# Linear attention and two feed-forward layers on one core: all attention tiles ahead of the first softplus, on one PSUM bank each

## The chip, the core and the metric

The kernel runs on one core of a Trainium2 chip. The metric is the device time of one execution in microseconds. The kernel before takes 881.84 us (median of 3 runs, 880.49 to 882.64).

## What is computed

```python
kv  = einsum('bhsd,bhse->bhde', k, v)      # b=4, h=8, s=576, d=64
o   = einsum('bhsd,bhde->bhse', q, kv)
o   = o / sqrt(mean(o*o, axis=-1) + 1e-6) * g_norm
x   = o.transpose(0, 2, 1, 3).reshape(2304, 512)
x   = softplus(x @ w_in1) @ w_out1         # 512 -> 2048 -> 512
out = elu(x @ w_in2) @ w_out2              # 512 -> 2048 -> 512
```

All in float32. The norm needs a reciprocal square root for each token and head.

## The kernel before, in words

The 2304 tokens are 6 blocks of 384. The 16 chunks of hidden units are taken in quarters of four. A *slot* is one pair of token blocks with one pair of chunks: 7 products (Strassen's scheme) of 6 matmuls each, 42 in all (`product`, line 695), written to PSUM tags `h` (2 banks), `m` and `o` (1 each). ScalarE and VectorE copy and add the parts, apply the activation (`slot_act`) and split the result into a high and a low part (tile `G`). The output pieces (`slot_piece`, lines 879 to 881, always three matmuls together) of a group of two slots run during the two slots that follow. Each layer has 24 slots.

A slot's first operand is made from the block's 7 sums (`operands`, line 648 on ScalarE, and `low_part`, line 660 on VectorE). Tag `sx` has room for 7 of these operand tiles. Each is also written out to memory (a *spill*, line 665) and loaded again in the later quarters. The weights come as raw words (line 269), are converted (`conv`, lines 278 to 298) and split (`split`, `split_pair`, `split_sums`, lines 305 to 363).

Attention makes the token blocks. `kv_strand` loads k and v (lines 385 and 387) into parts of `acc_sb` and multiplies them (line 396). Block 0 is made by four `pair_strand`s, the other tokens by 15 `tile_strand`s of 128 tokens; both go through `attention` (lines 451 to 511): load q (line 458), products with kv into a PSUM bank (line 467), squares on ScalarE (line 473), row sums on VectorE (line 482), a reciprocal root, a multiply (line 489), transposes on TensorE (line 504), and a scaled copy into `acc_sb` (line 509).

The root of the four pairs uses ScalarE's Ln and Exp and a Newton step of four small VectorE instructions (`rsqrt`). When the last pair is through, ScalarE's table is changed to that of softplus, which has no Ln and Exp; so the 15 tiles take their root from integer arithmetic (`rsqrt_pool`: a seed on VectorE, lines 438, 441 and 443, and three Newton rounds of four GpSimd instructions, lines 446 to 449, reckoned as `12 * 150` ns). The tiles of block 1 (`direct`) keep one bank of tag `acc` from the products to the transposes; the 12 others copy the products to the q tile (line 476), give the bank of tag `o` back, and take it again for the transposes.

What sets the order: `Order.run` is a list scheduler that runs while the program is built. Each strand yields its next step with the engines it may run on, an estimate of its cost in ns, and what it needs; the step that can start first is issued, and a strand with a smaller key may hold others back (by at most `WAIT` = 300 ns, or 200 ns). So every engine has a fixed order, laid down from estimates. Three steps may go to VectorE or GpSimd: lines 293, 319 and 357 (with 360). Where TensorE would be idle before slot 1, `warm` puts dummy matmuls (line 932). All DMAs are issued by SyncE, in the order of the plan.

Of the kernel before, what the change touches and what calls it, by code (L numbers as in the profile page):

```python
# [16 lines left out]
P = 128  # L17

# [30 lines left out]
class Order:  # L49
# [119 lines left out]
def linear_attention_then_two_ffns(  # L169
# [21 lines left out]
    nc = tc.nc  # L191
# [56 lines left out]
    def on(engine):  # L248
        return {DVE: nc.vector, POOL: nc.gpsimd, ACT: nc.scalar}[engine]

# [13 lines left out]
    def conv(i):  # L264
# [27 lines left out]
        e = yield ((DVE, dve(512) + 90), (POOL, pool(512), BIAS_I)), []  # L292
        on(e).tensor_tensor(c, c, r, op=ALU.add)
# [11 lines left out]
    def split(i, n):  # L305
# [19 lines left out]
    def split_pair(i, n):  # L325
# [4 lines left out]
        yield ((DVE, dve(256)),), [ring("c"), ring("r"), ("split", n), ("q", i + 1)]  # L330
# [13 lines left out]
        order.add(order.now, split_sums(layer, fc, ct, ct_h, rt, rt_h))  # L344
        yield from split(i + 1, n + 1)

    def split_sums(layer, fc, ct, ct_h, rt, rt_h):
        yield ((ACT, act(512)),), [ring("wx")]
        wx, wx_h = sbuf("wx", 2, f"wx{layer}_{fc}", (P, 2, 3, 256), F32R)
# [6 lines left out]
        e = yield ((DVE, dve(512)), (POOL, pool(512), BIAS_W)), []  # L356
        on(e).tensor_sub(wx[:, 1, 0::2, :], ct, f32(wx)[:, 0, 0::2, :])
        drop(ct_h)
        e = yield ((DVE, dve(256)), (POOL, pool(256), BIAS_W)), []
        on(e).tensor_sub(wx[:, 1, 1, :], rt[:, :256], f32(wx)[:, 0, 1, :])  # L360
        drop(rt_h)
        wx_t[layer, fc] = (wx, wx_h)
        mark("wx", layer, fc)


# [6 lines left out]
    def stage(b, c):  # L372

        return NB - NP + c if b < 2 else NB - 2 + c % 2

    def kv_strand(b, c):
        t = acc_sb[stage(b, c)]
        n, r = 4 * 2 * D2, S - 4 * P
        before = [
            ("kvmm", *k)  # L380
            for k in ((b0, c0) for b0 in range(B) for c0 in range(NP))
            if k < (b, c) and stage(*k) == stage(b, c)
        ]
        yield ((DMA, dma(4 * n * P)),), before
# [4 lines left out]
        tag = ("o", "acc", "m")[min(b, 2)]  # L389
# [13 lines left out]
        mark("kvmm", b, c)  # L403
        f = kvf[b % 2][:, c, :]
# [10 lines left out]
    ROOM = {"sx": 7, "wx": 2, "gx": 3}  # L415

    def rsqrt(ms, r, u, m, last):

        yield ((ACT, 100),), []
        nc.scalar.activation(r, ms, AF.Ln, scale=1.0 / D, bias=EPS)  # L420
        nc.vector.tensor_scalar(m, ms, 1.0 / D, EPS, op0=ALU.mult, op1=ALU.add)
        order.free[DVE] += 75
        yield ((ACT, 100),), []
        nc.scalar.activation(r, r, AF.Exp, scale=-0.5)
        if last:
            load_set(SOFTPLUS_SET)
        yield ((DVE, 75),), []
        nc.vector.scalar_tensor_tensor(u, r, -0.5, m, op0=ALU.mult, op1=ALU.mult)
        yield ((DVE, 75),), []
        nc.vector.tensor_mul(u, u, r)  # L430
        yield ((DVE, 75),), []
        nc.vector.scalar_tensor_tensor(r, u, 1.5, r, op0=ALU.add, op1=ALU.mult)

    def rsqrt_pool(ms, r, u, m):


        yield ((DVE, 75),), []
        nc.vector.tensor_scalar(m, ms, 1.0 / D, EPS, op0=ALU.mult, op1=ALU.add)
        yield ((DVE, 75),), []
        ub, rb = u.bitcast(U32), r.bitcast(U32)  # L440
        nc.vector.tensor_scalar(ub, m.bitcast(U32), 1, None, op0=ALU.logical_shift_right)
        yield ((DVE, 75),), []
        nc.vector.tensor_scalar(rb, ub, -1.0, float(0x5F3759DF), op0=ALU.mult, op1=ALU.add)
        yield ((POOL, 12 * 150),), []
        for _ in range(3):
            nc.gpsimd.tensor_mul(u, r, r)  # L446
            nc.gpsimd.tensor_mul(u, u, m)  # L447
            nc.gpsimd.tensor_scalar(u, u, -0.5, 1.5, op0=ALU.mult, op1=ALU.add)  # L448
            nc.gpsimd.tensor_mul(r, r, u)  # L449

    def attention(nm, load, products, n, tag, direct, parts):

# [4 lines left out]
        y = q.rearrange("p c t -> p (c t)")[:, :n]  # L457
# [3 lines left out]
            ring(tag),  # L461
# [7 lines left out]
        po = po[:, :n]  # L469
# [10 lines left out]
        small, small_h = sbuf("small", 3, f"small{nm}", (P, 4, H))  # L480
# [14 lines left out]

        if direct:
            yield ((PE, n // P * 109),), [("ident",)]
            pt, pt_h = bank, po_h
        else:
            yield ((PE, n // P * 109),), [ring(tag), ("ident",)]  # L500
            pt, pt_h = psum(tag, f"pt{nm}")
        for i in range(n // P):
            s = slice(i * P, (i + 1) * P)
            nc.tensor.transpose(pt[:, s], y[:, s], ident)
        drop(q_h)
        j, pt, x = parts(pt[:, :n])
        old = [("kvmm", b, c) for b in range(B) for c in range(NP) if stage(b, c) == j]
        yield ((ACT, act(n, True) + 90),), [("gn",), *old]
        nc.scalar.activation(x, pt, AF.Copy, scale=gn)  # L509
        drop(pt_h)  # L510
        mark("x", nm)

    def pair_strand(c):
# [12 lines left out]
        return attention(("pair", c), load, products, T, "acc", True, parts)  # L526

    def tile_strand(t):
# [20 lines left out]
        early = t < 2 * TT  # L549
        return attention(t, load, products, DM, "acc" if early else "o", early, parts)  # L550
# [107 lines left out]
    def low_part(layer, p, o, t, x, x_h):  # L658
# [48 lines left out]
    def slot_h(s, pieces):  # L707
# [40 lines left out]
        a, a_h = k["A"]  # L748
        order.add(key - URGENT, copy("ca", "hj", 1, 0))
# [37 lines left out]
    def softplus(s, b, h, a, ready):  # L787
        if a:
# [105 lines left out]
    BIAS_W = -1000  # L894
    BIAS_I = -400
# [5 lines left out]
    W_LEAD2 = 12  # L901
    A_LEAD = 12
    A_STEP = 1.2
    KV_LEAD = 2
    FIRST = -12
    CONV0 = -19.95
# [18 lines left out]
    def warm():  # L925

        p, p_h = psum("h", "warm")
        while entry[0] < base(1):
            yield ((PE, pe(P, 4)),), []
            if entry[0] < base(1):  # L930
                a = ident if ("x", ("pair", 0)) in order.marks else kvf[1][:, 0, :]
                nc.tensor.matmul(p[:, -P:], a, a, start=True, stop=True)
# [105 lines left out]
```

## Time and profile before

| | |
|---|---|
| median of the runs | 881.84 us |
| the profiled execution | 881.4 us |
| its span, first to last instruction | 879.6 us |
| TensorE busy | 832.4 us (95%) |
| VectorE busy | 619.0 us (70%) |
| ScalarE busy | 460.3 us (52%) |
| GpSimd busy | 66.3 us (8%) |
| mean granted TensorE clock | 0.979 |

In the profile PE is TensorE, PEld its weight loads, DVE is VectorE, ACT is ScalarE, POOL is GpSimd and SP is SyncE. Busy time is the time in which an instruction of the engine ran. Matmuls overlap, so their mean duration is longer than the distance from one to the next. The clock is granted as a share of 2.4 GHz; its two levels are 1.2 and 2.4 GHz.

### The profile page before, as it was taken

Reading aid. Unit: us, or ns where it says so; the run is one execution under the profiler, and the core shown is the slowest. Engines: PE = TensorE matmul, PEld = TensorE weight load, DVE = VectorE, ACT = ScalarE, POOL = GpSimd, SP = SyncE. Lnnn points to the kernel's source line nnn. Section 1 sums busy time; section 2 is a strip of 40 time slices with the busy share of each in tenths; the row PEclk is TensorE's granted clock in tenths of the full one; section 3 lists DMA queues with packets and bytes.
Section 4 is the critical chain, followed back from the end, with each engine's and each line's share of the span. In section 5 each row is a group of like instructions: output and inputs, shape, how many; then the busy total and the mean of one; then the engine's idle time right before and its main releaser. Section 6 shows DMA issues by size and latency. Waiting matters only on the chain.

```text
span 879.6 us, 12592 instructions
## 1 busy us (share of the span) xinstructions
PE 832.4 (95%) x4732; PEld 779.2 (89%) x4732; DVE 619.0 (70%) x1061; ACT 460.3 (52%) x781; POOL 66.3 (8%) x199
## 2 busy tenths in 40 slices
PE   7876687999999999999998999999999999999998
PEld 6775576999999999999997988888898888888887
DVE  4675676967636984589449999878559984995444
ACT  3564465666424553356235757676456643664431
POOL 0235544000000000000000000000000000000000
PEclk9996788999999999999999999999999999999999
DMA  6976262675664585377432765768538655744802
GB/s 204 316 265 241 87 263 92 266 254 181 237 251 147 213 336 195 120 281 288 175 139 85 287 242 189 278 213 307 193 115 307 225 213 184 280 156 151 310 37 107
DMA packets 43708, 185.36 MB, mean 211 GB/s; under 512 B 4992, under 2 KB 7808, under 8 KB 43648
## 3 DMA queue, kind: packets, MB, share of 16 engines
q1 hardware_dynamic: 43648, 184.57, 58.5%
q8 instruction: 37, 0.61, 0.3%
q14 instruction: 23, 0.19, 0.1%
HBM read 146.80 MB, written 37.75 MB: 210 GB/s over the span
## 4 chain that ended last, share of the span: by engine, by line
PE 79%; DVE 8%; POOL 6%; issue 2%; DMA 2%; ACT 2%; SPq 0%; POOLq 0%; DVEq 0%
PE A L695 20%; PE acc L880 14%; PE acc L881 14%; PE acc L879 14%; PE B L695 10%; PE C L695 5%; DVE x L660 2%; POOL small L447 2%; POOL small L449 2%; DMA acc_sb<-kv 2%; POOL small L446 1%; POOL small L448 1%; DVE q L489 1%; DVE acc_sb L642 1%; DVE acc_sb L569 1%
## 5 line engine op out<-in xcount | busy, mean ns | idle before, releaser
L879 PE MATMUL acc<-G,whi 128*128 128x384 f32 x384 | 129.6, 338 | 0.0
L881 PE MATMUL acc<-G,whi 128*128 128x384 f32 x384 | 128.9, 336 | 0.0
L880 PE MATMUL acc<-G,wlo 128*128 128x384 f32 x384 | 128.9, 336 | 0.0
L695 PE MATMUL A<-x,wx 128*128 128x384 f32 x576 | 118.1, 338 | 4.5 <-ACT x L648 2.6
L881 PE MATMUL acc<-wlo,G 128*128 128x512 f32 (+1 forms) x292 | 114.9, 393 | 0.0
L695 PE MATMUL A<-x,whi 128*128 128x384 f32 x384 | 113.2, 335 | 1.7 <-DVE x L660 1.7
L880 PE MATMUL acc<-whi,G 128*128 128x512 f32 (+1 forms) x292 | 114.4, 392 | 0.0
L879 PE MATMUL acc<-whi,G 128*128 128x512 f32 (+1 forms) x292 | 112.7, 386 | 0.0
L695 PEld LDWEIGHTS A<-x,wx 128*128 128x128 f32 x576 | 102.1, 189 | 10.9 <-ACT x L648 4.1
L733 DVE TENSOR_TENSOR hj<-hj,C 128x384 f32<-128x384 f32 x48 | 26.5, 553 | 71.6 <-PE C L695 71.3
L733 DVE TENSOR_TENSOR hk<-hk,B 128x384 f32<-128x384 f32 x48 | 26.5, 551 | 67.7 <-PE B L695 66.0
L695 PEld LDWEIGHTS A<-x,whi 128*128 128x128 f32 x384 | 70.7, 188 | 3.8 <-DVE x L660 2.0
L879 PEld LDWEIGHTS acc<-G,whi 128*128 128x128 f32 x384 | 72.7, 189 | 0.4 <-DVE acc_sb L569 0.2
L880 PEld LDWEIGHTS acc<-G,wlo 128*128 128x128 f32 x384 | 72.6, 189 | 0.0
L881 PEld LDWEIGHTS acc<-G,whi 128*128 128x128 f32 x384 | 72.5, 189 | 0.0
L315 ACT CAST whi<-q 128x512 fp32r<-128x512 f32 x64 | 39.6, 618 | 57.4 <-DVE q L297 32.6
L881 PEld LDWEIGHTS acc<-wlo,G 128*128 128x128 f32 x292 | 54.7, 187 | 11.3
L695 PE MATMUL A<-x,wlo 128*128 128x384 f32 x192 | 64.4, 335 | 0.0
L569 DVE TENSOR_TENSOR acc_sb<-acc_sb,acc 128x384 f32<-128x384 f32 (+1 forms) x108 | 62.3, 596 | 1.6
L695 PE MATMUL C<-x,whi 128*128 128x384 f32 x192 | 58.5, 346 | 3.3 <-ACT acc_sb L509 3.3
L879 PEld LDWEIGHTS acc<-whi,G 128*128 128x128 f32 x292 | 54.9, 188 | 6.0
L880 PEld LDWEIGHTS acc<-whi,G 128*128 128x128 f32 x292 | 54.8, 188 | 6.0
(151 smaller groups left out, 1594.2 us busy)
## 6 DMA issues: line engine op xcount, KB each, us to landing
x<-spill SPq DMA_DIRECT2D x126, 768.0 KB, 5.9
raw<-w SPq DMA_DIRECT2D x64, 512.0 KB, 5.5
spill<-x SPq DMA_DIRECT2D x42, 768.0 KB, 5.3
acc_sb<-kv SPq DMA_DIRECT2D x16, 512.0 KB, 5.4
out<-o SPq DMA_DIRECT2D x17, 256.0 KB, 2.0
q<-qt SPq DMA_DIRECT2D x15, 256.0 KB, 2.7
acc_sb<-kv_rest SPq DMA_DIRECT2D x16, 64.0 KB, 4.6
out<-o SPq DMA_DIRECT2D x2, 128.0 KB, 1.7
```

Source lines behind the costliest of these rows:

```text
L315: nc.scalar.copy(hi, q)
L446: nc.gpsimd.tensor_mul(u, r, r)
L447: nc.gpsimd.tensor_mul(u, u, m)
L448: nc.gpsimd.tensor_scalar(u, u, -0.5, 1.5, op0=ALU.mult, op1=ALU.add)
L449: nc.gpsimd.tensor_mul(r, r, u)
L569: nc.vector.tensor_add(a, a, p)
L660: nc.vector.tensor_sub(t[:, 2:, :], x, f32(t)[:, :2, :])
L695: nc.tensor.matmul(bank[:, :T], w, x, start=start and i == 0, stop=stop and i == len(seq) - 1, skip_group_check=True,)
L733: nc.vector.tensor_add(to, to, bank[:, :T])
L879: nc.tensor.matmul(a, l[0], r[0], start=(u == 0), stop=False)
L880: nc.tensor.matmul(a, l[1], r[0], start=False, stop=False)
L881: nc.tensor.matmul(a, l[0], r[1], start=False, stop=(u == QF - 1))
```

## The change

- All 19 tiles of attention take one path: Ln and Exp on ScalarE, then one Newton step of five GpSimd instructions (reckoned as `5 * 280` ns). The integer seed and the three rounds are gone. ScalarE's table is changed to softplus only when all 19 have their Exp issued; every softplus stands behind that.
- Every tile keeps one bank of tag `acc` (4 banks) from the products to the copy out. The copy to the q tile is gone; the q tile is free after the products, and the multiply reads PSUM and writes a tile of the `G` ring.
- k and v of batches 2 and 3 are loaded into the `gx` ring (3 tiles) and not into `acc_sb`; the kv products use tags `o` and `m` in turn.
- The attention strands get keys below those of the slots (`t - 20`), the first operands -14.5, weight chunks 2 and 3 -7.5. The spill of an operand gets a key of at least 1.
- Lines 293, 319, 357 and 360 run on VectorE alone.
- The dummy matmuls go on to slot 7 and are written to unused columns of the open slot's bank. The loads of later weights have other leads (8, and 12 more for some, where it was 12). The ring of `wx` is claimed earlier in `split_pair`.

The core of the diff:

```diff
@@ conv @@
-        e = yield ((DVE, dve(512) + 90), (POOL, pool(512), BIAS_I)), []
-        on(e).tensor_tensor(c, c, r, op=ALU.add)
+        yield ((DVE, dve(512) + 90),), []
+        nc.vector.tensor_tensor(c, c, r, op=ALU.add)
...
@@ split @@
-        e = yield ((DVE, dve(512)), (POOL, pool(512), BIAS_W)), [ring(f"wlo{half}")]
+        yield ((DVE, dve(512)),), [ring(f"wlo{half}")]
...
@@ kv_strand @@
+    def kv_room(b, c):
+        if b < 2:
+            return acc_sb[NB - NP + c], None
+        return sbuf("gx", ROOM["gx"], f"kv_sb{b}_{c}", (P, T * KC))
...
-        tag = ("o", "acc", "m")[min(b, 2)]
+        tag = "om"[c % 2]
...
@@ attention @@
-        po, po_h = psum(tag, f"po{nm}")
-        bank = po
+        bank, po_h = psum("acc", f"po{nm}")
         for b, c, rows, cols, lhs in products:
-            nc.tensor.matmul(po[rows, cols], lhs(q), kvf[b % 2][:, c, :], start=True, stop=True)
+            nc.tensor.matmul(bank[rows, cols], lhs(q), kvf[b % 2][:, c, :], start=True, stop=True)
+        drop(q_h)
...
-        if not direct:
-            yield ((ACT, act(n, True)),), []
-            nc.scalar.copy(y, po)
-            drop(po_h)
-            po = y
...
-        if isinstance(nm, tuple):
-            yield from rsqrt(ms, r, u, m, nm[1] == NP - 1)
-        else:
-            yield from rsqrt_pool(ms, r, u, m)
-        yield ((DVE, dve(n)),), []
+        yield ((ACT, 100),), []
+        nc.scalar.activation(r, ms, AF.Ln, scale=1.0 / D, bias=EPS)
+        yield ((ACT, 100),), []
+        nc.scalar.activation(r, r, AF.Exp, scale=-0.5)
+        roots.append(nm)
+        yield ((POOL, 5 * 280),), []
+        nc.gpsimd.tensor_scalar(m, ms, 1.0 / D, EPS, op0=ALU.mult, op1=ALU.add)
+        nc.gpsimd.tensor_mul(u, r, r)
+        nc.gpsimd.tensor_mul(u, u, m)
+        nc.gpsimd.tensor_scalar(u, u, -0.5, 1.5, op0=ALU.mult, op1=ALU.add)
+        nc.gpsimd.tensor_mul(r, r, u)
+        yield ((DVE, dve(n)),), [ring("G")]
+        y, y_h = sbuf("G", 4, f"y{nm}")
...
@@ low_part @@
+        order.rekey(max(order.now, SPILL))
         yield ((DMA, dma(P * 4 * T * 4)),), []
         nc.sync.dma_start(spilled[layer, p, o], f32(t))
...
@@ softplus @@
+        if s == 0 and a:
+            yield ((ACT, 1300),), [lambda: len(roots) == TILES]
+            load_set(SOFTPLUS_SET)
+            mark("softplus")
+        ready = [*ready, ("softplus",)]
...
-    W_LEAD2 = 12
-    A_LEAD = 12
-    A_STEP = 1.2
+    W_LEAD2 = 8
     KV_LEAD = 2
-    FIRST = -12
-    CONV0 = -19.95
+    FIRST = -14.5
+    SECOND = -7.5
+    SPILL = 1
+    WARM_SLOTS = 7
...
@@ warm @@
-        while entry[0] < base(1):
+        while entry[0] < base(WARM_SLOTS):
...
+                nc.tensor.matmul(
+                    (chain[0] if chain else p)[:, -P:], a, a, start=not chain, stop=not chain, skip_group_check=True
+                )
...
@@ the strands' keys @@
-            return n - (W_LEAD if n < base(FP * NPAIR) else W_LEAD2)
+            if n < base(FP * NPAIR):
+                return n - W_LEAD
+            return n - W_LEAD2 - (3 * W_LEAD if half and fc % QF < 2 else 0)
...
-            order.add(tile_key(t), tile_strand(t))
+            order.add(t - 20, tile_strand(t))
...
-                order.add(tile_key(b * S // P) - KV_LEAD + 0.1 * c, kv_strand(b, c))
+                order.add(b * S // P - 20 - KV_LEAD + 0.1 * c, kv_strand(b, c))
```

## Rows read from the trace of the kernel before

**Rows 1.** Windows: us, busy of PE, PEld, DVE, ACT, POOL, then clock, DMA, GB/s

```profile
0.00:30.00 30.00, 22.24 (x239) 18.93 (x240) 13.66 (x39) 12.68 (x32) 1.97 (x7) 0.94 0.73 237
70.00:80.00 10.00, 3.11 (x30) 2.16 (x29) 5.19 (x9) 4.44 (x9) 5.70 (x21) 0.59 0.42 146
0.00:160.00 160.00, 121.17 (x928) 107.94 (x929) 103.04 (x206) 84.50 (x164) 59.96 (x195) 0.88 0.60 206
160.00:200.00 40.00, 40.00 (x233) 40.00 (x232) 29.92 (x50) 26.11 (x45) 1.89 (x1) 1.00 0.75 282
200.00:300.00 100.00, 100.00 (x579) 100.00 (x578) 65.68 (x113) 47.31 (x84) 0.00 (x0) 1.00 0.60 214
470.00:530.00 60.00, 54.63 (x293) 50.70 (x292) 58.15 (x94) 38.05 (x60) 0.00 (x0) 1.00 0.60 229
```

**Rows 2.** Windows again, PE and PEld alone: line 695's matmuls, then line 879's

```profile
0.00:160.00 160.00, 36.92 (x159) 31.36 (x160) 0.88 0.60 206
...
0.00:160.00 160.00, 10.26 (x27) 5.65 (x27) 0.88 0.60 206
```

**Rows 3.** Waits of VectorE, 0 to 160 us: total, times, longest

```profile
DVE q L489 <- POOL small L449: 27.9, 15, 2.6
```

**Rows 4.** Chain of waits, 0 to 160 us, its shares by line

```profile
by line: issue 9.5%; POOL small L447 8.6%; POOL small L449 8.5%; DMA acc_sb<-kv 8.5%; POOL small L446 7.3%; POOL small L448 7.0%; DVE q L489 5.9%; DVE x L660 5.8%; DVE small L482 3.0%; PE pt L504 2.5%; DMA q('pair', 3)_265<-qt 1.9%; DVE q L
```

**Rows 5.** Timeline: GpSimd, one tile's first and last root step; VectorE, its multiply

```profile
39.69 0.19 POOL L446 TENSOR_TENSOR small<-small 128x8 f32<-128x8 f32 x1
...
43.08 0.20 POOL L449 TENSOR_TENSOR small<-small 128x8 f32<-128x8 f32 x1
...
43.31 0.69 DVE L489 TENSOR_TENSOR q<-po,small 128x512 f32<-128x512 f32 x1 [1.23 <-POOL small L449]
```

**Rows 6.** Groups of VectorE, 0 to 160 us: count, busy us, mean ns, idle before

```profile
L489 DVE TENSOR_TENSOR q<-q,small 128x512 f32<-128x512 f32 x12 | 11.4, 954 | 22.2 <-POOL small L449 22.2
L293 DVE CUSTOM_DVE_ANT_0 c<-c,r 128x1024 uint16<-128x1024 uint16 x7 | 4.8, 692 | 0.6
...
L438 DVE TENSOR_SCALAR small<-small 128x8 f32<-128x8 f32 x15 | 3.4, 237 | 0.1
L443 DVE TENSOR_SCALAR small<-small 128x8 uint32<-128x8 uint32 x15 | 3.1, 207 | 0.2
...
L441 DVE TENSOR_SCALAR small<-small 128x8 uint32<-128x8 uint32 x15 | 2.8, 198 | 0.1
...
L489 DVE TENSOR_TENSOR q<-po,small 128x512 f32<-128x512 f32 x3 | 2.1, 692 | 5.7 <-POOL small L449 5.7
...
L428 DVE SCALAR_TENSOR_TENSOR small('pair', 0)_188<-small('pair', 0)_188 128x6 f32<-128x6 f32 x1 | 0.2, 166 | 1.2 <-ACT small('pair', 0)_188 L424 1.2
```

**Rows 7.** Groups of GpSimd, 0 to 160 us

```profile
L447 POOL TENSOR_TENSOR small<-small 128x8 f32<-128x8 f32 x45 | 13.2, 294 | 3.5
...
L319 POOL TENSOR_TENSOR wlo<-q,whi 128x512 fp32r<-128x512 f32 x3 | 3.8, 1270 | 34.0 <-ACT whi L315 34.0
L293 POOL TENSOR_TENSOR c<-c,r 128x512 uint32<-128x512 uint32 x3 | 3.8, 1269 | 3.2 <-DVE c L288 3.2
L357 POOL TENSOR_TENSOR wx<-t,wx 128x512 fp32r<-128x512 f32 x2 | 2.5, 1270 | 0.0
```

**Rows 8.** Timeline of SyncE's queue

```profile
58.40 6.59 SPq L665 DMA_DIRECT2D spill<-x  x6
```

**Rows 9.** DMA issues: count, KB each, median us to landing

```profile
acc_sb<-kv SPq DMA_DIRECT2D x16, 512.0 KB, 5.4
...
q<-qt SPq DMA_DIRECT2D x15, 256.0 KB, 2.7
```

**Rows 10.** Timeline: first products of pairs 0 and 3, pair 3's last step

```profile
8.63 0.91 PE L467 MATMUL po('pair', 0)_160<-kvf,q('pair', 0)_150 128*128 128x128 f32 x6 [1.64 <-DMA q('pair', 0)_150<-qt]
...
20.86 0.91 PE L467 MATMUL po('pair', 3)_282<-kvf,q('pair', 3)_265 128*128 128x128 f32 x6 [1.46 <-DMA q('pair', 3)_265<-qt]
...
26.27 0.58 ACT L509 ACTIVATE acc_sb<-po('pair', 3)_282,gn 128x384 f32<-128x384 f32 x1 [0.76 <-PE po('pair', 3)_282 L504]
```

More of the change, by code (lines that the diff above doesn't have):

```diff
@@ L246, in f32 @@
         return t.bitcast(F32)
-    def on(engine):
-        return {DVE: nc.vector, POOL: nc.gpsimd, ACT: nc.scalar}[engine]
     ident = const.tile([P, P], F32, name="ident")
@@ L329, in split_pair @@
         order.add(order.now, split(i, n))
-        yield ((DVE, dve(256)),), [ring("c"), ring("r"), ("split", n), ("q", i + 1)]
+        need = [ring("c"), ring("r"), ring("wx"), ("split", n), ("q", i + 1)]
+        yield ((DVE, dve(256)),), need
+        wx = sbuf("wx", ROOM["wx"], f"wx{layer}_{fc}", (P, 2, 3, 256), F32R)
         ct, ct_h = sbuf("c", 1, f"t13_{layer}_{fc}", uses=2)
@@ L343, in split_pair, with split_sums @@
         drop(qa_h)
-        order.add(order.now, split_sums(layer, fc, ct, ct_h, rt, rt_h))
+        order.add(order.now, split_sums(layer, fc, *wx, ct, ct_h, rt, rt_h))
         yield from split(i + 1, n + 1)
-    def split_sums(layer, fc, ct, ct_h, rt, rt_h):
-        yield ((ACT, act(512)),), [ring("wx")]
-        wx, wx_h = sbuf("wx", 2, f"wx{layer}_{fc}", (P, 2, 3, 256), F32R)
+    def split_sums(layer, fc, wx, wx_h, ct, ct_h, rt, rt_h):
+        yield ((ACT, act(512)),), []
         ct = ct.rearrange("p (two n) -> p two n", two=2)
@@ L363, in split_sums @@
         mark("wx", layer, fc)
+    roots = []
+    TILES = NP + NTT - TT
     made_of = [
@@ L370, in linear_attention_then_two_ffns @@
     made_of[0] += [("pair", c) for c in range(NP)]
-    def stage(b, c):
-        return NB - NP + c if b < 2 else NB - 2 + c % 2
+    ROOM = {"sx": 7, "wx": 2, "gx": 3}
+    def kv_room(b, c):
+        if b < 2:
+            return acc_sb[NB - NP + c], None
+        return sbuf("gx", ROOM["gx"], f"kv_sb{b}_{c}", (P, T * KC))
     def kv_strand(b, c):
-        t = acc_sb[stage(b, c)]
         n, r = 4 * 2 * D2, S - 4 * P
[L379 to L384, printed above, removed]
+        yield ((DMA, dma(4 * n * P)),), ([], [("kvmm", 0, c)], [ring("gx")])[min(b, 2)]
+        t, t_h = kv_room(b, c)
         nc.sync.dma_start(t[:, :n], kv[b, c].rearrange("p n t d -> p (n t d)"))
@@ L403, in kv_strand @@
         mark("kvmm", b, c)
+        if t_h:
+            drop(t_h)
         f = kvf[b % 2][:, c, :]
@@ L413, in kv_strand, with attention @@
         mark("kv", b, c)
[L415 to L451, printed above, removed]
+    def attention(nm, load, products, n, parts):
         h = n // D
@@ L494, in attention @@
         drop(small_h)
[L496 to L501, printed above, removed]
+        yield ((PE, n // P * 109),), [("ident",)]
         for i in range(n // P):
             s = slice(i * P, (i + 1) * P)
[L504 to L507, printed above, removed]
+            nc.tensor.transpose(bank[:, s], y[:, s], ident)
+        drop(y_h)
+        j, pt, x = parts(po)
+        old = [("kvmm", 1, j - NB + NP)] if j >= NB - NP else []
         yield ((ACT, act(n, True) + 90),), [("gn",), *old]
         nc.scalar.activation(x, pt, AF.Copy, scale=gn)
-        drop(pt_h)
+        drop(po_h)
         mark("x", nm)
@@ L525, in pair_strand @@
         ]
-        return attention(("pair", c), load, products, T, "acc", True, parts)
+        return attention(("pair", c), load, products, T, parts)
     def tile_strand(t):
@@ L548, in tile_strand @@
             s = e
-        early = t < 2 * TT
-        return attention(t, load, products, DM, "acc" if early else "o", early, parts)
+        return attention(t, load, products, DM, parts)
     def block_sum(layer, q, j, i, w0, w1, p, p_h):
@@ L748, in slot_h @@
         a, a_h = k["A"]
+        chain[:] = [a]
         order.add(key - URGENT, copy("ca", "hj", 1, 0))
@@ L900, in linear_attention_then_two_ffns @@
     W_LEAD = 4
-    W_LEAD2 = 12
-    A_LEAD = 12
-    A_STEP = 1.2
+    W_LEAD2 = 8
     KV_LEAD = 2
-    FIRST = -12
-    CONV0 = -19.95
+    FIRST = -14.5
+    SECOND = -7.5
+    SPILL = 1
+    WARM_SLOTS = 7
+    chain = []
     def main():
@@ L927, in warm @@
         p, p_h = psum("h", "warm")
-        while entry[0] < base(1):
+        while entry[0] < base(WARM_SLOTS):
             yield ((PE, pe(P, 4)),), []
-            if entry[0] < base(1):
-                a = ident if ("x", ("pair", 0)) in order.marks else kvf[1][:, 0, :]
-                nc.tensor.matmul(p[:, -P:], a, a, start=True, stop=True)
-        drop(p_h)
+            a = ident if ("x", ("pair", 0)) in order.marks else kvf[1][:, 0, :]
+            if chain and p_h:
+                drop(p_h)
+                p_h = None
+            if entry[0] < base(WARM_SLOTS):
+                nc.tensor.matmul(
+                    (chain[0] if chain else p)[:, -P:], a, a, start=not chain, stop=not chain, skip_group_check=True
+                )
     def setup():
```

33 lines of the change are left out of this document (11 added, 22 removed).

## The prediction

> **What bounds the kernel now.** I looked first at long windows [rows 1]. From 200 to 300 us TensorE is busy all the time (100.00 us, 579 matmuls, 172.7 ns each); from 160 to 200 us it is too. From 0 to 160 us it is busy 121.17 us at a mean clock of 0.88. How much of that is layer work? The same window with only the two matmul lines of the layers [rows 2] has 159 matmuls of line 695 and 27 of line 879; lines 880 and 881 run as often as 879, so 159 + 3 x 27 = 240 matmuls, at 172.7 ns 41.5 us of work. The first 160 us thus hold 41.5 us of layer work, and the rest runs nearly without a gap. Call T the moment from which TensorE runs through, and w the layer work done by then. The span is T - w + 761.1 us (719.6 us after 160, plus 41.5). Only T - w can move much.
>
> Why does the start take so long? VectorE is busy 103.04 of the 160 us [rows 1], so it idles 57.0 us; 27.9 us of that, in 15 waits, is line 489 waiting for the last GpSimd step of the root [rows 3]. The chain of the stage shows the same [rows 4]: lines 446 to 449 on GpSimd are 31.4% of it. The timeline of one tile [rows 5] tells why: twelve dependent steps from 39.69 to 43.28 us, 3.6 us, where the planner reckons 12 x 150 ns = 1.8 us. So the planner queues line 489 on VectorE about 1.8 us too early, and everything behind it on that queue stands still.
>
> **The change, part by part.** VectorE carries most of the start, so I count it.
> - Newton: the three seed instructions per tile go (3.4 + 3.1 + 2.8 = 9.3 us [rows 6]), as do four VectorE steps for each of four pairs (16 x 0.166 = 2.7 us, from one of them). GpSimd does 5 steps for each of 19 tiles instead of 12 for 15: 95 against 180. Five take 5/12 of 3.6 = 1.5 us, and the planner now reckons 1.4, so the queue is built on a true price. The 27.9 us of waits therefore go. Two ScalarE steps (Ln, Exp) stand ahead of them; they are in the pairs' path below.
> - One bank: the last multiply reads PSUM (692 ns) and not the SBUF copy (954 ns, x12) [rows 6]: 3.1 us off VectorE. The copy to SBUF is gone from ScalarE.
> - No large GpSimd work: three line 319, three line 293 and two line 357 come to VectorE [rows 7]; at 692 ns each [rows 6] this adds 5.5 us.
>
> Sum for VectorE: 103.0 - 9.3 - 2.7 - 3.1 + 5.5 = 93.4 us of work for the state now reached at 160 us.
>
> How much of the other idle time, 57.0 - 27.9 = 29.1 us, stays? In the first 30 us VectorE is busy 13.66 us [rows 1], so 16.3 us is the wait for the first loads and chains, and stays. The remaining 12.8 us is bounded from both sides: all of it stays, and the state is reached at 93.4 + 29.1 = 122.5 us, 37.5 us earlier; or VectorE packs as it does at 470 to 530 us (58.15 of 60, 0.97 [rows 1]), and the state is reached at 30 + 79.7/0.97 = 112.2 us, 47.8 us earlier. I take half the 12.8 us: up to four tiles are in flight, but in a fixed order. That gives 116.1 us, 43.9 us earlier, and a span of 835.7 us. The profiled execution took 881.4 us, 1.8 over its span, and the median of the runs is 0.4 above that: 837.9, rounded to **838 us**.
>
> On the Newton steps the rows weigh like this: a GpSimd step takes 294 ns [rows 7], a small VectorE step 166 ns [rows 6], so GpSimd makes each tile's path longer by about 5 x 0.13 = 0.65 us, but takes 95 x 0.166 = 15.8 us off the engine that carries this stage. The Trainium skill, "GPSIMD Engine Reference", section "Engine selection", says the opposite of the edit: elementwise work belongs on VectorE, GpSimd being about twice as slow. By that rule the steps on VectorE would be better; by the rows they would add 15.8 us to the sum, so I follow the rows.
>
> Moved or added, at no cost in the sum:
> - The softplus gate. ScalarE reloads its table once all 19 roots are out; behind that reload stand slot 0's softplus, its G casts, and through its PSUM bank slot 2. Only two h banks exist, so w at the gate is two slots' 84 matmuls, 14.5 us. Cover: VectorE has the start's other work; without it rival 2 holds.
> - SyncE: now six spills, issued from 58.40 us on, hold its queue for 6.59 us [rows 8], with input loads behind them; the change puts the spills behind the input loads. In return, pair 1's operand tiles come free later: 7 x 768 KB at 282 GB/s [rows 1], about 20 us after the last load. It can cost from nothing to 10 us; I take nothing, since the loads should end well before the gate, and keep 10 for the range.
> - Later weight loads: hidden while TensorE is full (200 to 300 us). At the layer change TensorE already idles 5.4 us of 60 with VectorE at 58.15 [rows 1]; if the cover fails there, as much again is lost. I keep 6 us either way.
> - Dummy matmuls up to slot 7: they fill only gaps the planner sees. A gap that isn't there costs the length of the dummy; I take nothing.
>
> **The rivals.**
> 1. TensorE is fed as soon as the gate opens. The kv and q loads are 16 x 512 + 15 x 256 KB = 12.3 MB [rows 9]; at 237 to 282 GB/s [rows 1] 44 to 52 us. With the small loads, four weight loads and the last path of 6.7 us the gate opens near 65 us: 65 - 14.5 + 761.1 = 811.6, or **814 us**. Against it: slot 2 needs pair 1's operands, and VectorE must still make them, the G's and the output weights.
> 2. The gate is late and the backlog isn't hidden, or the clock falls. At 70 to 80 us, with TensorE busy 3.11 of 10 us, the granted clock was 0.59 [rows 1], so mostly the lower of its two levels. Then the 43.9 us of gain are half given back: about **860 us**. Dummies to slot 7 speak against. The Trainium skill, "TensorE: Matmul & The Clock Gate", section "HAM oscillation", warns that idle gaps of TensorE halve its clock; this row agrees.
> 3. **Slower.** The place is the tile's path through the PSUM bank. A pair's path, alone, runs from 20.86 to 26.85 us, 6.0 us [rows 10]; with the root on GpSimd 6.7. If TensorE's fixed order lets each tile's transposes block the next tile's products, 19 tiles follow one another: 8.6 + 19 x 6.7 = 136 us for the gate, 136 - 14.5 + 761.1 = 882.6, or **885 us**. It decides from 6.5 us per tile on (gate at 133 us). 8.6 is when the first pair's products start [rows 10]. For it: line 489's 15 waits [rows 3] show what a wrong order costs here, and 19 tiles now share one ring of banks. Against it: four banks allow a tile every 6.7/4 = 1.7 us, and the planner's price of the root is now near the true one.
> 4. The change doesn't do what it says: keys are only preferences, and the planner lets slots pass ahead as now. Then only the Newton price changes and other waits take its place: **880 us**.
>
> **How the numbers follow.** Forecast (826 to 852) 0.50; rival 1 (805 to 826) 0.17; rival 2 (852 to 876) 0.17; rival 3 0.12; rival 4 0.04. A measurement of this kernel can tell about 0.3% from no change, 2.6 us. Faster is the first three and part of rival 4: 0.85; the same 0.03; slower 0.12. The range takes the forecast with its bounds and the 10 and 6 us kept, and rivals 1 and 2 but for their outer ends (0.03), and leaves out rivals 3 and 4 (0.16): 806 to 872.
>
> **What would show it.** Right: the waits of line 489 for GpSimd fall from 27.9 us to under 8; VectorE is above 0.85 from 30 us on; the table reload stands at 60 to 80 us; TensorE is full from about 115 us; 200 to 300 us looks as before. Wrong: a reload after 100 us; long waits of TensorE for bank releases in the tiles (rival 3); layer-work matmuls far apart right after the reload, waiting for operand tiles or spills (rival 2); or new gaps near the layer change.

## The result, and the profile after

The kernel after takes 844.07 us (median of 4 runs, 843.19 to 844.97). The kernel before took 882.24 us beside it, so the ratio is 0.9569 (95%: 0.9549 to 0.9589), 4.3% faster. The profiled execution took 843.19 us, with a span of 841.1 us. The forecast was 838, in a range of 806 to 872.

The engines over the whole span, from the page of the profile:

```profile
PE 824.6 (98%) x4814; PEld 778.9 (93%) x4814; DVE 600.2 (71%) x986; ACT 466.1 (55%) x826; POOL 29.9 (4%) x101
```

The windows after, with the columns of [rows 1]; the second, third and last are new:

```profile
0.00:30.00 30.00, 24.53 (x281) 21.48 (x281) 9.32 (x17) 13.09 (x40) 7.07 (x31) 1.00 0.84 274
30.00:126.00 96.00, 88.73 (x722) 84.20 (x721) 81.66 (x128) 69.99 (x151) 22.78 (x70) 0.98 0.70 252
0.00:128.00 128.00, 115.25 (x1012) 107.67 (x1013) 92.98 (x147) 84.45 (x192) 29.85 (x101) 0.99 0.74 256
...
200.00:300.00 100.00, 100.00 (x579) 100.00 (x578) 66.69 (x118) 44.53 (x76) 0.00 (x0) 1.00 0.59 216
...
450.00:510.00 60.00, 59.34 (x316) 55.55 (x315) 56.07 (x90) 41.98 (x67) 0.00 (x0) 1.00 0.50 187
```

From 200 to 300 us TensorE does the same as before: 579 matmuls in 100 us, as in [rows 1]. The gain lies at the start and at the layer change. For the start, the layer work in the first 160 us, counted as in [rows 2] (PE and PEld alone, line 650, then line 840):

```profile
0.00:160.00 160.00, 50.04 (x246) 43.48 (x246) 0.99 0.75 264
...
0.00:160.00 160.00, 20.32 (x60) 11.39 (x61) 0.99 0.75 264
```

That is 246 + 3 x 60 = 426 matmuls, 186 more than before; at 172.7 ns they are 32.1 us. Counted in steps of 1 us, the 240 matmuls of before's first 160 us are reached at 128 us. At the layer change TensorE idled 5.37 of 60 us (470 to 530, [rows 1]); now it idles 0.66 of 60 (450 to 510), 4.7 us less. The spans differ by 38.5 us: 32.1 + 4.7, and 1.7 us that I don't assign.

VectorE's waits from 0 to 130 us (total, times, longest):

```profile
DVE small L433 <- ACT sq L429: 7.9, 6, 4.6
DVE small('pair', 0)_179 L433 <- ACT sq('pair', 0)_166 L429: 6.4, 1, 6.4
DVE x L614 <- ACT x L602: 3.8, 3, 2.1
DVE small('pair', 1)_224 L433 <- ACT sq('pair', 1)_211 L429: 3.7, 1, 3.7
DVE y L450 <- POOL small L446: 3.1, 6, 0.7
DVE wlo L307 <- ACT whi L303: 2.4, 2, 1.7
```

Line 450 is the multiply that was line 489. Its 27.9 us of waits for the root [rows 3] are now 3.1, with 1.0 and 0.7 for two pairs 4.8 in all. What VectorE now waits for most is ScalarE.

The timeline of ScalarE at the gate (start, duration):

```profile
80.55 0.21 ACT L439 ACTIVATE small<-small 128x8 f32<-128x8 f32 x1
80.78 1.28 ACT L226 ACT_TABLE_LOAD   x1
```

The last root's Exp is out at 80.76 us and the table reload follows at once. The chain from 0 to 160 us, by line:

```profile
by line: PE A L650 14.9%; PE A L898 9.2%; DMA acc_sb<-kv 7.9%; PE acc L841 6.5%; DMA kv_sb<-kv 6.5%; PE B L650 6.5%; PE acc L840 6.5%; PE acc L842 6.4%; DMA raw<-w 4.2%; PE po L422 4.1%; DMA q<-qt 4.1%; PE C L650 3.9%; PE kv L388 3.3%; PE p
```

GpSimd's four lines, 31.4% of it before [rows 4], are gone from the top. In their place stand TensorE's layer work (lines 650 and 840 to 842), the dummies (line 898, 9.2%) and the loads of k and v (14.4%). SyncE's queue around it (start, time the queue was held):

```profile
66.14 1.81 SPq L487 DMA_DIRECT2D q<-qt  x2
...
84.47 16.84 SPq L620 DMA_DIRECT2D spill<-x  x7
```

The last q tiles are asked for at 66 us, and seven spills stand together behind them.

### The profile page after: what moved, and what is told of

It reads as the page before. It is cut to its first block, busy times and chain, and to the rows that moved or that the text cites. A ratio compares the mean times of both kernels' runs of the same rounds, so it can differ in the third digit from the quotient of the medians.

```text
span 841.1 us, 12584 instructions
## 1 busy us (share of the span) xinstructions
PE 824.6 (98%) x4814; PEld 778.9 (93%) x4814; DVE 600.2 (71%) x986; ACT 466.1 (55%) x826; POOL 29.9 (4%) x101
## 4 chain that ended last, share of the span: by engine, by line
PE 93%; DMA 4%; SPq 1%; ACT 1%; issue 0%; POOL 0%; DVE 0%; ACTq 0%; DVEq 0%
PE A L650 24%; PE acc L841 16%; PE acc L842 16%; PE acc L840 16%; PE B L650 12%; PE C L650 6%; PE A L898 2%; DMA acc_sb<-kv 1%; DMA kv_sb<-kv 1%; DMA raw<-w 1%; PE po L422 1%; DMA q<-qt 1%; PE kv L388 1%; PE po L459 0%; SPq L379 0%
## 5 line engine op out<-in xcount | busy, mean ns | idle before, releaser
L650 PE MATMUL B<-x,wx 128*128 128x384 f32 x288 | 58.2, 336 | 0.0
L303 ACT CAST whi<-q 128x512 fp32r<-128x512 f32 x64 | 39.7, 620 | 32.4 <-DVE q L285 14.3
```

Source lines behind the costliest of these rows:

```text
L303: nc.scalar.copy(hi, q)
L650: nc.tensor.matmul(bank[:, :T], w, x, start=start and i == 0, stop=stop and i == len(seq) - 1, skip_group_check=True,)
```

## The experiments

Each ran beside the kernel before (medians 882.19, 881.75 and 881.51 us in the three groups). The last column is where 240 layer matmuls are reached in the profiled execution.

| kernel | median us | ratio (95%) | 240 at, us |
|---|---|---|---|
| before | 882.24 | 1 | 160 |
| after | 844.07 | 0.9569 (0.9549 to 0.9589) | 128 |
| b_price | 872.20 | 0.9888 (0.9873 to 0.9902) | 148 |
| a_twelve_gate | 854.96 | 0.9697 (0.9682 to 0.9712) | 141 |
| a_twelve_nogate | 861.85 | 0.9772 (0.9756 to 0.9787) | 148 |
| a_dve_newton | 859.38 | 0.9735 (0.9720 to 0.9751) | 145 |
| a_no_kv1 | 841.37 | 0.9549 (0.9530 to 0.9568) | 129 |
| a_warm1 | 845.83 | 0.9582 (0.9555 to 0.9609) | 133 |
| a_lead | 853.38 | 0.9682 (0.9667 to 0.9698) | 132 |
| a_spill | 850.42 | 0.9657 (0.9633 to 0.9680) | 135 |
| a_two_banks | 847.25 | 0.9609 (0.9595 to 0.9624) | 131 |
| a_pool | 856.75 | 0.9715 (0.9699 to 0.9732) | 134 |
| a_conv0 | 842.12 | 0.9553 (0.9531 to 0.9575) | 130 |
| a_best | 837.64 | 0.9513 (0.9487 to 0.9539) | 124 |

### b_price: before, with the true price of the root

```diff
-        yield ((POOL, 12 * 150),), []
+        yield ((POOL, 12 * 300),), []
```

> The kernel before, with one number changed: the planner reckons the root's twelve GpSimd steps at 12 x 300 ns and no longer at 12 x 150. No instruction is added or removed, only the fixed order may differ. Theory A (the wrong price was the loss: VectorE stood with the multiply at the head of its queue): the 27.9 us of waits of line 489 for GpSimd fall below 8 us and the time falls by 15 to 28 us, to 854 to 867 us. Rival B (twelve dependent steps are too long, whatever is reckoned): the wait goes elsewhere and the time stays at 876 to 888 us. Rival C (the gain is made by putting all attention first and by one bank a tile): also 876 to 888 us, but with the waits of line 489 gone.

Measured: 872.20 us, 10.0 less, between what the two sides expected. Waits of VectorE in the first 160 us:

```profile
DVE q L489 <- POOL small L449: 11.7, 10, 1.5
...
DVE small L482 <- ACT sq L473: 4.5, 3, 2.6
DVE wlo L319 <- ACT whi L315: 4.5, 3, 3.3
DVE s L634 <- ACT acc_sb L509: 4.1, 3, 3.1
```

The waits for the root fall from 27.9 to 11.7 us, 16.2 less, and the start is 12 us earlier. The price alone, with not one instruction changed, is worth about a quarter of the change's 38 us. A part of what it frees comes back as waits for ScalarE: 13.1 us in the three groups shown, where the kernel before has 5.6 at the same lines.

### a_twelve_gate and a_twelve_nogate: after, with the long root of before

The 15 tiles have the integer seed on VectorE and twelve GpSimd steps again, priced at `12 * 290`. The first keeps the gate for all 19 roots. The second has it for the pairs alone, as before, and its multiply writes the q tile.

```diff
-        yield ((POOL, 5 * 280),), []
+        if not isinstance(nm, tuple):
+            yield from rsqrt_pool(ms, r, u, m)
+            roots.append(nm)
+        else:
+            yield from rsqrt_short(nm, ms, r, u, m)
...
-            yield ((ACT, 1300),), [lambda: len(roots) == TILES]
+            yield ((ACT, 1300),), [lambda: len(roots) == NP]
```

> The changed kernel, with the 15 tiles' root as before the change (seed on VectorE, twelve GpSimd steps) but reckoned at its true length, 12 x 290 ns; the softplus still waits for all 19 roots. Theory A (price) and C (order): the order stays good; VectorE has 9.3 us more work and each tile's path is 2 us longer, so 846 to 856 us. Rival B (length): GpSimd's 15 x 3.6 = 54 us stand on the path again, the table reload comes after 95 us and the time is 865 us or more.

> As the run with twelve steps, and the softplus waits for the four pairs alone, so slots may go on while tiles are still made; the multiply writes the q tile. It tells what the gate costs or gives. If the gate delays the slots (rival 2 of the prediction): 5 to 15 us faster than the run with the gate. If the gate is hidden behind VectorE's work: within 4 us of it. If the layers' work between the tiles spoils their order, as in the kernel before: slower by 5 us or more.

Measured: 854.96 and 861.85 us. The first lies in the 846 to 856 that was expected where the root's length is only a part of the gain, and below the 865 of the other side, though the reload came after 95 us, as that side had said. With b_price this makes a chain of steps: the price 10.0 us, everything else but the root 17.2 (872.20 to 854.96), the short root 10.9 (854.96 to 844.07). So some 27 of the 38 us do not need the short root. Nor is the 10.9 the root's length alone, as the short root also takes the three seed instructions off VectorE. Up to the 240th matmul (141 us) VectorE is busy 98.76 us in a_twelve_gate and 92.98 (128 us) in after, so 5.8 of those 13 us are VectorE's work and 7.2 its idle time.

The reload stands at 97.49 us in the first and at 67.53 in the second. Still the second is 6.9 us slower: an open gate did not bring the start forward. That is against my fear that a late gate costs. It doesn't show that a gate helps, as the second differs in the q tile too: it holds that tile until the transposes, and TensorE's wait for q grows to 8.8 us, from 1.9 with the gate (first 160 us):

```profile
PE po L453 <- DMA q<-qt: 8.8, 10, 2.2
```

### a_dve_newton: the five steps on VectorE

```diff
-        yield ((POOL, 5 * 280),), []
-        nc.gpsimd.tensor_scalar(m, ms, 1.0 / D, EPS, op0=ALU.mult, op1=ALU.add)
+        yield ((DVE, 5 * 200),), []
+        nc.vector.tensor_scalar(m, ms, 1.0 / D, EPS, op0=ALU.mult, op1=ALU.add)
...
```

> The changed kernel with the five Newton steps of each of the 19 tiles on VectorE and not on GpSimd. By the prediction's sum VectorE carries the start and gets 95 x 0.166 = 15.8 us more: 852 to 860 us. By the rule that elementwise work belongs on VectorE: each tile's path is about 0.65 us shorter and the time is the same or less, 838 to 846 us. If the start is set by the loads and not by VectorE: within 3 us of 844.

Measured: 859.38 us, 15.3 more than after. The prediction had 95 x 0.166 = 15.8 us for this. The steps on VectorE, 0 to 160 us, and on GpSimd in the kernel after:

```profile
L445 DVE TENSOR_SCALAR small<-small 128x8 f32<-128x8 f32 x15 | 2.6, 171 | 0.5
L446 DVE TENSOR_TENSOR small<-small 128x8 f32<-128x8 f32 x15 | 2.5, 167 | 0.5
```

```profile
L444 POOL TENSOR_TENSOR small<-small 128x8 f32<-128x8 f32 x15 | 6.6, 437 | 1.2
L445 POOL TENSOR_SCALAR small<-small 128x8 f32<-128x8 f32 x15 | 5.0, 336 | 1.3
```

Each step is twice as fast on VectorE (167 to 171 ns against 336 to 437), and yet the kernel is slower. Its window up to the 240th matmul:

```profile
0.00:145.00 145.00, 130.19 (x1120) 121.53 (x1121) 104.11 (x239) 85.51 (x194) 0.70 (x6) 0.96 0.65 225
```

VectorE is busy 11.1 us more than in after (104.11 against 92.98), and it idles 5.9 us more: at the head of its queue it now waits 8.6 us for ScalarE's Exp, where GpSimd did that before. So VectorE's work is the larger part of the loss and not all of it, and that 15.3 comes so near to 15.8 is partly luck. The Trainium skill, "GPSIMD Engine Reference", section "Engine selection", which puts elementwise work on VectorE, is right here about the speed of one instruction and wrong about the kernel.

### a_spill: the spills not put behind the inputs

```diff
-    SPILL = 1
+    SPILL = -100
```

> The changed kernel without the new key for the spills: they stand in SyncE's queue where the operands are made, ahead of input loads. Theory (spills ahead of loads delay the tiles): the table reload comes 6 to 15 us later than 80.8 us and the time is 6 to 14 us longer, 850 to 858 us. Rival (loads are early enough, and pair 1's operand tiles come free earlier): within 3 us of 844 or faster.

Measured: 850.42 us, 6.4 more, inside the expected 6 to 14. But the reload, which should have come later, stands at 80.22 us. SyncE's queue says what happened:

```profile
46.12 9.99 SPq L620 DMA_DIRECT2D spill<-x  x6
...
66.06 3.82 SPq L487 DMA_DIRECT2D q<-qt  x3
```

Six spills hold the queue for 10 us, with inputs behind them. VectorE then runs dry (windows of this kernel, then of after):

```profile
60.00:70.00 10.00, 9.92 (x109) 8.75 (x108) 3.83 (x8) 5.91 (x14) 2.53 (x9) 1.00 0.73 261
80.00:100.00 20.00, 18.96 (x156) 18.30 (x156) 15.16 (x25) 12.14 (x20) 1.72 (x9) 1.00 0.21 77
```

```profile
60.00:70.00 10.00, 8.85 (x72) 8.13 (x71) 8.50 (x15) 6.88 (x19) 5.29 (x19) 1.00 0.93 346
80.00:100.00 20.00, 19.30 (x136) 18.84 (x136) 18.34 (x27) 17.61 (x29) 2.44 (x6) 1.00 0.54 218
```

VectorE does 3.83 us of work from 60 to 70 us where it does 8.50 in after, and 15.16 against 18.34 from 80 to 100. At 60 us it had been 1.6 us ahead of after (34.85 against 33.30 us of work); at 100 it is 6.5 behind (62.79 against 69.32), and the start is 7 us later. The tiles' roots catch up in time for the gate; VectorE's lost time doesn't come back. So the key of the spills is worth 6.4 us, by VectorE's supply and not by the gate.

### a_lead: the weights' old lead

```diff
-    W_LEAD2 = 8
+    W_LEAD2 = 12
...
-            return n - W_LEAD2 - (3 * W_LEAD if half and fc % QF < 2 else 0)
+            return n - W_LEAD2
```

> The changed kernel with the lead of the later weight loads as before the change (12 for all). It tells where the 4.7 us at the layer change went (TensorE idled 5.4 us of 60 before and 0.7 us after). Theory (the new leads did it): TensorE idles 4 to 6 us at the layer change again, and the time is 4 to 8 us longer, 848 to 852. Rival (VectorE work moved from GpSimd, or the shift of the whole kernel, did it): within 2 us of 844.

Measured: 853.38 us, 9.3 more. 4 us of it is at the start; the rest is at the layer change. The window there (this kernel, then after) and the timeline of the stall:

```profile
440.00:520.00 80.00, 72.92 (x383) 69.09 (x382) 75.02 (x119) 53.96 (x85) 0.00 (x0) 0.96 0.57 217
```

```profile
440.00:520.00 80.00, 79.34 (x423) 74.67 (x423) 75.17 (x116) 56.66 (x91) 0.00 (x0) 1.00 0.61 235
```

```profile
463.45 0.69 PE L842 MATMUL acc<-G,whi 128*128 128x384 f32 x1 [7.07 <-DVE G L802]
463.94 0.52 PE L840 MATMUL acc<-G,whi 128*128 128x384 f32 x1
464.26 0.52 PE L841 MATMUL acc<-G,wlo 128*128 128x384 f32 x1
...
468.94 0.33 PE L841 MATMUL acc<-G,wlo 128*128 128x384 f32 x1
469.12 0.33 PE L842 MATMUL acc<-G,whi 128*128 128x384 f32 x1
```

TensorE waits once, for 7.07 us, for one G of VectorE, which is as busy here as in after (75.02 and 75.17 us). So it is not the amount of VectorE's work in this stretch; that its order differs is my reading, and was not traced. The leads are what took the 4.7 us off the layer change, a term that the prediction had put at zero with 6 us either way.

### a_pool: large operations on GpSimd allowed again

```diff
-        yield ((DVE, dve(512) + 90),), []
-        nc.vector.tensor_tensor(c, c, r, op=ALU.add)
+        e = yield ((DVE, dve(512) + 90), (POOL, pool(512), BIAS_I)), []
+        on(e).tensor_tensor(c, c, r, op=ALU.add)
...
-        yield ((DVE, dve(512)),), [ring(f"wlo{half}")]
+        e = yield ((DVE, dve(512)), (POOL, pool(512), BIAS_W)), [ring(f"wlo{half}")]
```

> The changed kernel with the integer add and the low part of the weights allowed on GpSimd again, with the planner's prices and biases of before. Theory (GpSimd's large operations hold VectorE and the Newton steps up; a small VectorE step took 1.27 us beside one in the kernel before): VectorE instructions beside them get longer, and the time is 2 to 10 us longer, 846 to 854. Rival (each such operation takes 0.69 us off the engine that carries the start): 2 to 5 us faster.

Measured: 856.75 us, 12.7 more than after; the direction was expected, the size was not (846 to 854). The planner now sends far more to GpSimd than in the kernel before. Groups over the whole span, this kernel and then after:

```profile
L317 POOL TENSOR_TENSOR wlo<-q,whi 128x512 fp32r<-128x512 f32 x63 | 94.0, 1494 | 429.2 <-ACT whi L313 425.0 <-PE B L660 4.0
L291 POOL TENSOR_TENSOR c<-c,r 128x512 uint32<-128x512 uint32 x26 | 42.2, 1623 | 125.2 <-DVE c L286 89.5 <-ACT G L810 32.6 <-ACT acc_sb L527 3.1
...
L356 DVE TENSOR_TENSOR wx<-t,wx 128x512 fp32r<-128x512 f32 x16 | 21.4, 1340 | 5.8 <-ACT wx L350 5.8
L624 DVE TENSOR_TENSOR x<-acc_sb,x 128x768 fp32r<-128x768 f32 x36 | 39.2, 1105 | 1.4 <-ACT x L612 1.3
L698 DVE TENSOR_TENSOR hk<-hk,B 128x384 f32<-128x384 f32 x48 | 26.4, 550 | 80.2 <-PE B L660 69.1 <-ACT q L278 10.1 <-ACT hk L688 1.1
```

```profile
L346 DVE TENSOR_TENSOR wx<-t,wx 128x512 fp32r<-128x512 f32 x16 | 11.0, 685 | 0.0
L614 DVE TENSOR_TENSOR x<-acc_sb,x 128x768 fp32r<-128x768 f32 x36 | 33.9, 953 | 3.9 <-ACT x L602 3.8
L688 DVE TENSOR_TENSOR hk<-hk,B 128x384 f32<-128x384 f32 x48 | 26.5, 553 | 75.1 <-PE B L650 65.2 <-ACT q L268 9.4
```

GpSimd's operation, 1270 ns in [rows 7], takes 1494 and 1623 ns. And VectorE's own slow down: the sum of the weights from 685 to 1340 ns, line 614's from 953 to 1105. The one whose second input is in PSUM does not (553 and 550). The Trainium skill, "SBUF — State Buffer", section "Who interferes with whom", says that a VectorE instruction with two SBUF inputs and a GpSimd instruction that reads SBUF use one port and that the later one is held up entirely; the three groups agree. So an operation given to GpSimd costs VectorE a part of what it saves, and here all of it. Up to the 240th matmul (134 us) GpSimd had taken 12 of them, some 8 us of VectorE's work at 0.69 us each, and VectorE was still busy 93.67 us, against 92.98 in after. Over the whole span it was busy 602.5 us, against 600.2. The start is 6 us later, by VectorE's idle time, whose cause was not traced; the layer change loses 2.4 us (TensorE busy 76.95 of 80 us from 440 to 520), and the other 4 us are not assigned.

### a_warm1, a_two_banks, a_no_kv1, a_conv0: four parts with little in them

```diff
-    WARM_SLOTS = 7
+    WARM_SLOTS = 1
```

> The changed kernel with dummy matmuls only up to slot 1, as before the change. Theory: the dummies keep the granted clock of the start at 0.98; without them it falls below 0.9 between 60 and 120 us and the time is 2 to 8 us longer. Rival (the dummies stand in the way: 50 of them took 5.85 us from 90.95 us on, ahead of the first output piece): 1 to 4 us faster.

Measured: 845.83 us, 1.8 more, with overlapping intervals. Without the dummies the granted clock from 60 to 120 us was 0.89 and not 1.00, and the start in the profiled execution was 5 us later. The medians don't settle whether that is worth anything: by the two intervals, from nothing to some 5 us.

In a_two_banks each tile copies its products out, gives the bank back and takes one again for the transposes:

```diff
+        yield ((ACT, act(n, True)),), [ring("G")]
+        y, y_h = sbuf("G", 4, f"y{nm}")
+        nc.scalar.copy(y[:, :n], po)
+        drop(po_h)
...
-        yield ((PE, n // P * 109),), [("ident",)]
+        yield ((PE, n // P * 109),), [ring("acc"), ("ident",)]
+        bank, po_h = psum("acc", f"pt{nm}")
```

> The changed kernel with the two-bank path for all 19 tiles: ScalarE copies the products to SBUF, the bank is given back, the multiply reads SBUF, and a bank of the same ring is taken again for the transposes. By the prediction's count this costs ScalarE about 19 x 0.6 us = 11 us and VectorE 15 x 0.26 = 4 us. Theory (VectorE sets the start): 2 to 6 us longer, 846 to 850. Rival (the bank is held for the whole path and the tiles wait for it): 3 us faster or more. Rival (ScalarE is as near its limit as VectorE): 8 us longer or more.

Measured: 847.25 us, 3.2 more, inside the expected 2 to 6, but not for the expected reason. The multiply reads SBUF here, and takes no longer than from PSUM in after (689 ns):

```profile
L454 DVE TENSOR_TENSOR y<-y,small 128x512 f32<-128x512 f32 x15 | 10.3, 689 | 6.3 <-POOL small L452 6.1
0.00:131.00 131.00, 119.04 (x1047) 111.25 (x1048) 93.08 (x150) 91.50 (x208) 30.58 (x101) 0.99 0.72 250
```

VectorE's work up to the 240th matmul (131 us) is that of after, 93.08 us against 92.98; what grew is its idle time, by 2.9 us. The 954 ns that the prediction took from the kernel before is a mean of two kinds. Line 489 there, with its shortest, median and longest time in ns, and the first of its three long ones (start, duration):

```profile
L489 DVE TENSOR_TENSOR q<-q,small x12: 691/693/1741, 68.7 to 153.5; 128x512 f32<-128x512 f32 x12
...
89.06 1.73 DVE L489 TENSOR_TENSOR q<-q,small 128x512 f32<-128x512 f32 x1 [0.58 <-POOL small L449]
...
88.98 1.26 POOL L357 TENSOR_TENSOR wx<-t,wx 128x512 fp32r<-128x512 f32 x1
```

Nine of the twelve took 0.69 us. The three long ones, at 89.06, 99.09 and 124.06 us, each began within 0.1 us of a large GpSimd operation, which is what a_pool shows. So the 3.1 us came with the large operations that left GpSimd, and not with the bank.

```diff
-        nc.sync.dma_start(t[:, :n], kv[b, c].rearrange("p n t d -> p (n t d)"))
+        if b != 1:
+            nc.sync.dma_start(t[:, :n], kv[b, c].rearrange("p n t d -> p (n t d)"))
```

> The changed kernel without the eight loads of k and v of batch 1 (4 x 512 and 4 x 64 KB, 2.3 MB, about 8 us at 274 GB/s): batch 1 is multiplied with batch 0's k and v, which still lie there. The planner still reckons the loads, so the order stays. Theory L (up to 54 us the input loads set the pace, and VectorE's idle time in the start is theirs): 4 to 8 us faster, 836 to 840 us, and VectorE is busy more than 9.3 us in the first 30. Rival V (VectorE's work sets the start whenever the loads land): within 2 us of 844.

This run leaves out the eight loads of k and v of batch 1, and nothing else. Measured: 841.37 us, 2.7 less, intervals overlapping, and the start no earlier (129 us). The 836 to 840 of the theory that the loads set the start did not come. The amount of input is not what the start waits for; the first weight load is issued at the same time as in after (14.37 and 14.20 us), so this run says nothing of its place in the queue.

That place is what a_conv0 moves, for the first chunk of weights alone:

```diff
-                k = FIRST - 2 if i < 2 else SECOND
+                k = (-19.95, FIRST - 2, SECOND, SECOND)[i]
```

> The changed kernel with the first weight chunk loaded and converted as early as before the change (key -19.95 and not -16.5). VectorE was busy only 9.3 us in the first 30 after the change, 13.7 before, because the first weights were loaded at 14.2 us instead of 1.8. Theory (this idle time is never made up, since VectorE carries the rest of the start): VectorE is busy 12 us or more in the first 30, and the time is 2 to 4 us shorter, 840 to 842. Rival (the load ahead of k, v and q delays the tiles by as much): within 1.5 us of 844 or longer.

Measured: 842.12 us, 2 less, not to be told from after. VectorE's work in the first 30 us rose from 9.32 to 11.39 us, but 240 matmuls were reached no sooner (130 us). Inconclusive by itself.

### a_best: earlier keys for the first weights and operands

```diff
-    H_KEY = 2
+    H_KEY = 3
...
-    FIRST = -14.5
-    SECOND = -7.5
+    FIRST = -15.5
+    SECOND = -10
...
-                k = FIRST - 2 if i < 2 else SECOND
+                k = (-19.95, FIRST - 2, SECOND, SECOND)[i]
```

> As the run with the first chunk early, and with the first operands (-15.5 for -14.5) and weight chunks 2 and 3 (-10 for -7.5) earlier, and the activations one key later. Meant as the version that beats both. If VectorE's order in the start has slack left: 836 to 841 us. If the start is packed as well as it can be: within 2 us of 844.

Measured: 837.64 us (837.30 to 841.42), 0.9513 of before with an interval that lies below that of after (upper end 0.9539 against 0.9549). Its windows:

```profile
0.00:30.00 30.00, 25.08 (x267) 22.03 (x268) 13.29 (x27) 13.16 (x35) 4.67 (x22) 0.94 0.84 255
...
440.00:520.00 80.00, 80.00 (x425) 75.17 (x424) 74.58 (x116) 57.58 (x94) 0.00 (x0) 1.00 0.59 227
```

VectorE does 13.29 us of work in the first 30 us, 4.0 more than in after and as much as before did (13.66); the start is 4 us earlier, and the last 0.66 us of idle time at the layer change are gone. Four keys moved together here; a_conv0 had one of them alone, and the other three were not tried apart.

## Why the prediction was right, and where its terms were off

- **The model of the span** held. Layer work in the first 160 us and a constant rest gave 32.1 us; the "constant" 761.1 us was 754.7 (681.1 us after 160, plus 73.6), by the layer change and the 1.7 us not assigned.
- **VectorE carries the start**: right. Its work up to the 240th matmul was to be 93.4 us and was 92.98. The seeds, the pairs' Newton, the multiply and the large operations come out as a sum; not each term stands. The multiply's 3.1 us was put down to PSUM, and a_two_banks shows it at 689 ns from SBUF too: the longer mean of before came from large GpSimd work beside it. For the Newton steps 15.8 us was forecast and 15.3 measured, of which a part is idle time.
- **The 27.9 us of waits go**: right in the main, 4.8 stay where the sum has none. Five steps were to take 1.5 us; by their means they take 1.6, and single ones up to 1.0 us. b_price shows that the false price made about 16 of them and the rest needed the shorter root or the other order.
- **The other idle time** is the step that failed. I let 16.3 us stay in the first 30 us and half of 12.8 after, 22.7 together. VectorE idled 35.0 us in all (128 - 92.98), of which 4.8 are the waits for the root, so the other idle time was 30.2, past my bound of 29.1. So the state came at 128 us and not at 116.1, nor within 112.2 to 122.5. In the first 30 us VectorE idles 20.7 us, 18.6 without the root: 19 attention loads now stand ahead of the weights in SyncE's queue, and the first weight load is issued at 14.20 us where the kernel before issues it at 1.78. I had gone through the queue for the spills and not for this. The order that a_best gives takes 4 us of it back; moving the first weights alone (a_conv0) did not. Behind 30 us VectorE idles 14.3 us, 11.6 without the root, so 1.2 of the 12.8 went and not half. Of its waits from 30 to 128 us 10.9 us are for ScalarE (lines 602, 429, 303, 800 and 464). ScalarE took over two steps a root and is busy 69.99 of the 96 us from 30 to 126; I had costed its steps as path and not as load. That its load is the cause was read from the waits, and a_two_banks speaks against it as the only one: ScalarE is busy 7 us more there up to the 240th matmul (91.50 against 84.45), and VectorE's waits for it behind 30 us are 7.8 us and not 10.9, with 5.4 for the root. Load or order stays open.
- **The gate** at 60 to 80 us: it came at 80.78. TensorE is busy 10.00 of 10 us from 110 us on, with dummies (line 898) for 2.2 of the first ten; the last of them ran before 115 us, where I had said that TensorE is full. And VectorE is busy 0.85 of the time from 30 to 126 us. That the gate costs nothing, as forecast, fits with a_twelve_nogate, which opened it at 67.53 us and brought nothing forward, but isn't shown by it, as the q tile differs there too.
- **The spills**: at no cost behind the inputs, right; left where they were they would have cost 6.4 us, which the 0 to 10 us kept for them holds.
- **Later weight loads**: costed at zero with 6 us either way. They gave 4.7 us at the layer change, and a_lead takes that back and more. What in the leads does it was not traced.
- **Dummies**: nothing, within what the medians tell.
- **Large operations off GpSimd**: the sum has them as a cost of 5.5 us, and as a part of VectorE's work that held, with the multiply's 3.1 us to be set against it. As an account of the edit it was wrong in sign in this plan: allowing them again costs 12.7 us. I had priced GpSimd's side and the work saved, not the slowing of VectorE. The two kernels don't send the same operations there, so the 12.7 is a_pool's price and not that of the eight operations of [rows 7].

The forecast of 838 against 844 is thus partly luck: the start came 12 us late, and the layer change and the unassigned rest gave back 6.4. Of the rivals, 1 needed the start to follow the gate at 65 us (the gate came at 81, and TensorE's layer work was then not fed through, with 240 matmuls at 128). 2 fell with the clock, which was 0.98 from 30 to 126 us, and with a_warm1. 3 needed tiles one after another: the last of 19 roots was out at 80.8 us and not at 133. 4 fell with the timeline, all tiles before the reload. The parts tried one at a time (15.3, 12.7, 9.3, 6.4 and 3.2 us) don't add up to the change, as each makes the planner lay down another order.

## What to carry to other kernels

Where a program built from estimates sets every engine's order, compare its price of each step with the trace first: one wrong figure was worth 10 us of 882 here. Count the busy time of the engine that fills the stage, move small steps off it even to an engine half as fast, and for each queue that a step is moved past ask what now stands behind it, the first loads of another stage included. Look at the spread of a price and not only at its mean: 954 ns was nine times 0.69 us and three times 1.7. An idle allowance needs its own reading: list the waits that remain, by engine, before calling half of them gone.

## What had not been expected of the hardware

- VectorE's instructions with two inputs in SBUF took up to twice as long beside large GpSimd operations (685 to 1340 ns), those with an input in PSUM as long as before (a_pool). Line 282, with one input in SBUF, lengthened too: from 421 ns (line 272 in after) to 587, in the first 160 us.
- After the one stall of 7.07 us in a_lead, matmuls of 384 columns came 0.32 us apart until 467.46 us and 0.17 us apart from 467.90 on: some 4 us at the lower clock. By these distances the stall costs about 2 us more than its length, an estimate.
- The small GpSimd steps of the root ran at 272 to 437 ns in after by the means of their lines, at 197 to 263 by the medians. The long ones are those that meet a VectorE instruction with two inputs in SBUF. The timeline lists 20 that took over 0.3 us singly; each began during such an instruction or within 0.01 us of its start, and ended 0.05 to 0.07 us after it. So VectorE holds GpSimd up as well. One of the 20 (start, duration):

```profile
40.39 0.95 DVE L596 TENSOR_TENSOR acc_sb<-acc_sb,acc_sb 128x768 f32<-128x768 f32 x1
...
40.62 0.78 POOL L445 TENSOR_SCALAR small<-small 128x8 f32<-128x8 f32 x1
```
